# A gated recurrence feeding a SwiGLU block: the recurrence's output made transposed, and carried to the SwiGLU's operand by SBUF transfers

## The chip, the cores and the metric

The kernel runs on one core of a Trainium2 chip. The metric is the device time of one execution in microseconds (us). Five engines run side by side, each through its own instructions in order: TensorE (PE, with its weight loads shown as PEld), VectorE (DVE), ScalarE (ACT), GpSimd (POOL) and SyncE (SP), which here only issues DMA transfers.

## The reference, cut to what matters

```python
batch, n_heads, seq, head_dim = (4, 8, 768, 48)          # q, k, v, f_logit, float32
f = 1.0 / (1.0 + np.exp(-f_logit))
for t in range(S):
    state = f[:, :, t, :, None] * state + np.einsum('bhd,bhe->bhde', k[:, :, t], v[:, :, t])
    y[:, :, t] = np.einsum('bhd,bhde->bhe', q[:, :, t], state)
...
x = np.ascontiguousarray(attn_out.transpose(0, 2, 1, 3)).reshape(B * S, H * D)   # 3072 x 384
g = x @ w_gate                                            # 384 x 1536
silu = g * (1.0 / (1.0 + np.exp(-g)))
val = x @ w_val
return (silu * val @ w_out).astype(np.float32)            # 1536 x 384
```

The three weights arrive as 64-bit floats and are turned into 32-bit ones on the chip.

## The kernel before, in words

The sequence is cut into 6 chunks of 128 steps. A unit is one chunk of one batch; there are 24 units, chunk by chunk, 4 batches in each. For a unit the function `attention` does these things, with a `yield` between them:

- `fTp` (L462): 4 TensorE transposes of the gate logits, two heads at a time; ACT takes the sigmoid into `gates`.
- DVE runs a backward product scan (`tails`, L472) and prepares `starts`.
- `kTp`, `qTp` (L462): 8 transposes; DVE multiplies them by the scans into `kT` (L483) and `qT` (L487). A head occupies 48 of 64 rows: even heads rows 0 to 47, odd heads rows 64 to 111. POOL multiplies the state by the chunk's total decay into `decayed` (L491).
- `sc` (L499): the 128 x 128 score matrix of each head, two heads of a pair side by side in the rows of the array; DVE masks them into `A` (L501). `kt` (L506): 4 transposes of `kT`.
- `y` (L516, L519): for each pair of heads one product of `qT` with `decayed` (128 x 96) and two of `A` with `v` (128 x 48), summed in PSUM; ACT copies the 128 x 384 result into `x` (L522). `dS` (L526): eight products that give the state's update.
- `xTp` (L542): 3 transposes of `x`; ACT copies them into `xT` (L543), where features are rows and the 4 x 128 tokens of a chunk are columns.

A chunk of `xT` (512 tokens) is one block of the SwiGLU, `mlp`: for each of 12 slices of 128 hidden features a `gate` piece and a `val` piece of 3 matmuls each (L564), then 4 `down` pieces, one per batch, of 12 matmuls each (L580, tile `o`). An fp32 matmul shows as two matmul records and two weight loads, a transpose as one.

The first chunk's attention runs alone. After it, `take_turns` mixes the SwiGLU pieces of chunk c with the attention steps of chunk c + 1: after piece i it has issued the share i/n of the steps. `attention_steps` orders these steps so that two units overlap; `parts = [1, 2, 1, 1, 1]` says how many yields go into each of a unit's steps. In the first block `weights()` pieces are mixed in too: each fetches a piece of a 64-bit weight (SP), splits it (ACT) and joins it (DVE, L416 to L420). Where such program order leaves a choice, the tile framework's scheduler settles the order in each engine's queue. SP's queue also holds the loads of `f`, `k`, `q`, `v` of the unit three ahead, in order; outputs go by ACT's queue. PSUM has 4 banks for attention (`bank`) and 4 for the SwiGLU.

Of the kernel before, what the change touches and what calls it, by code (L numbers as in the profile page):

```python
# [9 lines left out]
FP32 = mybir.dt.float32  # L10
# [279 lines left out]
def short_path(ctx, tc, least, judge, q, k, v, f_logit, moe_w_gate, moe_w_val, moe_w_out, out):  # L290
# [26 lines left out]
    att = ctx.enter_context(tc.tile_pool(name="att", bufs=2))  # L317
    ffn = ctx.enter_context(tc.tile_pool(name="ffn", bufs=2))
# [5 lines left out]
    ident = const.tile([128, 128], FP32, tag="ident", name="ident")  # L324
# [51 lines left out]
    vt = {}  # L376
# [69 lines left out]
    xT = {}  # L446

    def rows_of(par):
        return slice(W * par, W * par + D)

    def bank(name):
        return aps.tile([128, 512], FP32, tag="a", name=name)

    def attention(u):
        b, c = units[u]
        fr, kr, qr = (raw[nm][u % NRAW] for nm in "fkq")
        gate, tail, start = (x[u % NROT] for x in (gates, tails, starts))

        def transposed(name, src):
            p = bank(name)  # L460
            for a in range(HP):
                nc.tensor.transpose(p[:, a * C:(a + 1) * C],  # L462
                                    src[:, 2 * a:2 * a + 2, :].rearrange("t r d -> t (r d)"), ident)
            return p.rearrange("p (a t) -> p a t", t=C)

        p = transposed("fTp", fr)
# [4 lines left out]
        n = HP * N1  # L471
# [14 lines left out]
        qT = att.tile([128, HP, C], FP32, tag="qT", name="qT")  # L486
        nc.vector.tensor_tensor(qT, qp, pairs(head)[:, :, 1:N1], ALU.mult)  # L487
# [15 lines left out]
        if c < NCH - 1:  # L503
            p = bank("kt")
# [3 lines left out]
            nc.scalar.copy(kt, p.rearrange("t (h d) -> t h d", d=W))  # L508
        yield


        y = bank("y")
        for a in range(HP):
            both = y[:, 2 * a * D:2 * (a + 1) * D]
            if c:
                nc.tensor.matmul(both, lhsT=qT[:, a, :], rhs=decayed[:, a, :, :].rearrange("p r d -> p (r d)"),  # L516
                                 start=True, stop=False, skip_group_check=True)
            for par in range(2):
                nc.tensor.matmul(both[:, par * D:(par + 1) * D], lhsT=A[:, par, a, :], rhs=vt[u][:, 2 * a + par, :],  # L519
                                 start=(c == 0), stop=True, skip_group_check=True)  # L520
        x = att.tile([128, DM], FP32, tag="x", name="x")
        nc.scalar.copy(x, y[:, 0:DM])  # L522
        if c < NCH - 1:
            p = bank("dS")
            for h in range(H):
                nc.tensor.matmul(p[W * (h % 2):W * (h % 2) + W, (h // 2) * D:(h // 2 + 1) * D],  # L526
                                 lhsT=kt[:, h, :], rhs=vt[u][:, h, :], start=True, stop=True)
# [7 lines left out]
        yield  # L535


        if b == 0:
            xT[c] = ffn.tile([128, KT, TB], FP32, tag="xT", name="xT", bufs=2)
        p = bank("xTp")  # L540
        for i in range(KT):
            nc.tensor.transpose(p[:, i * C:(i + 1) * C], x[:, i * 128:(i + 1) * 128], ident)  # L542
        nc.scalar.copy(xT[c][:, :, b * C:(b + 1) * C], p[:, 0:KT * C].rearrange("p (a t) -> p a t", t=C))  # L543
        yield

    def load_after(u):
# [3 lines left out]
    def attention_steps(c):  # L550

        runs = [attention(c * B + b) for b in range(B)]
        parts = [1, 2, 1, 1, 1]
        order = sorted((2 * b + s, b, n) for b in range(B) for s, n in enumerate(parts))
        return [lambda b=b, n=n: [next(runs[b]) for _ in range(n)] for _, b, n in order]


    def mlp(c):
        h = {}

        def product(w, j, name):
            p = fps.tile([128, 512], FP32, tag="m", name=name)[:, 0:TB]
            for i in range(KT):
                nc.tensor.matmul(p, lhsT=w[:, i, j * 128:(j + 1) * 128], rhs=xT[c][:, i, :],  # L564
                                 start=(i == 0), stop=(i == KT - 1))
            return p

        def gate(j):
            p = product(w_gate, j, "gate")
            h[j] = ffn.tile([128, TB], FP32, tag="h", name="h", bufs=NF + 1)  # L570
            nc.scalar.activation(h[j], p, AF.Silu)  # L571

        def val(j):
            p = product(w_val, j, "val")
            nc.vector.tensor_tensor(h[j], h[j], p, ALU.mult)  # L575

        def down(b):
            p = fps.tile([128, 512], FP32, tag="m", name="o")[:, 0:DM]
            for j in range(NF):
                nc.tensor.matmul(p, lhsT=h[j][:, b * C:(b + 1) * C], rhs=w_out[:, j, :],  # L580
                                 start=(j == 0), stop=(j == NF - 1))
            ob = ffn.tile([128, DM], FP32, tag="ob", name="ob", bufs=3)
            nc.scalar.copy(ob, p)  # L583
            t0 = b * S + c * C
            nc.scalar.dma_start(out=out[t0:t0 + C, :], in_=ob)

        return ([lambda j=j, f=f: f(j) for i in range(0, NF, 2) for f in (gate, val) for j in (i, i + 1)]
                + [lambda b=b: down(b) for b in range(B)])

    def take_turns(first, second):  # L590

        done = 0
        for i, f in enumerate(first):
            f()
            want = (i + 1) * len(second) // len(first)
            for g in second[done:want]:
                g()
            done = want
        for g in second[done:]:
            g()  # L600

    def weights():
        if fetches:
# [10 lines left out]
    mark = traced[-1]  # L614
    keep_warm(5)
    first = [attention(b) for b in range(B)]
    done = [0] * B

# [60 lines left out]
def kernel(  # L679
# [22 lines left out]
    def judge(bank):  # L702
# [46 lines left out]
```

## Time and profile before

| | |
|---|---|
| time, median of 3 runs | 729.62 us (729.58 to 729.69) |
| the profiled execution's own time | 729.66 us |
| its span (first to last instruction) | 727.9 us |
| granted TensorE clock, mean | 0.998 |
| busy: PE, PEld, DVE, ACT, POOL | 718.8, 415.8, 248.9, 185.2, 21.6 us |
| DMA | 38.34 MB, mean 53 GB/s |

A row of the groups view names the line, engine, operation, written and read tiles with their shape, and how many; then the busy time and the mean duration of one in ns; then the idle time of the engine before them and what ended it. A row of the timeline gives start and length in us; consecutive instructions of one kind are merged, and since matmuls are pipelined a merged row ends later than the next one starts. The time that a group takes on the path is therefore read from one row's start to the next row's start.

### The profile page before, as it was taken

What the parts mean: (1) busy time and instruction counts of PE and PEld (TensorE: products, weight loads), DVE (VectorE), ACT (ScalarE), POOL (GpSimd) and SP (SyncE); (2) the same over time, 40 slices, a digit from 0 to 9 for tenths busy, and PEclk for the clock granted to TensorE, in tenths of its full rate; (3) what the DMA queues carried; (4) which work ended last, traced back from release to release, by engine and by line L of the source; (5) the groups of instructions that cost most, each with busy time, mean ns of one, the idle gap of its engine ahead of it and who ended that gap; (6) DMA issues with size and microseconds to landing.
All of it is one profiled execution on the core that took longest, in us unless ns stands there. A gap on an engine that the chain in (4) does not pass through costs nothing.

```text
span 727.9 us, 7635 instructions
## 1 busy us (share of the span) xinstructions
PE 718.8 (99%) x3146; PEld 415.8 (57%) x3146; DVE 248.9 (34%) x405; ACT 185.2 (25%) x272; POOL 21.6 (3%) x43
## 2 busy tenths in 40 slices
PE   8999999999999999999999999999999999999997
PEld 6845555655555665555566555556555566544454
DVE  8799797024234003333202433311333320011100
ACT  2655473032212103323103213301223210100100
POOL 2000000000000000000000000000000000000000
PEclk9999999999999999999999999999999999999999
DMA  9988463112111002211101112010200000000000
GB/s 194 249 224 226 140 172 76 32 35 43 32 33 40 26 23 44 44 23 32 33 23 43 33 33 43 12 32 23 45 1 1 0 1 23 23 0 1 0 23 24
DMA packets 109772, 38.34 MB, mean 53 GB/s; under 512 B 100512, under 2 KB 103584, under 8 KB 109728
## 3 DMA queue, kind: packets, MB, share of 16 engines
q1 hardware_dynamic: 106272, 33.04, 19.5%
q10 hardware_dynamic: 3456, 4.72, 1.8%
q8 instruction: 27, 0.44, 0.2%
q14 instruction: 17, 0.14, 0.1%
HBM read 33.03 MB, written 4.72 MB: 52 GB/s over the span
## 4 chain that ended last, share of the span: by engine, by line
PE 97%; DVE 1%; ACT 1%; DMA 1%; SPq 0%; issue 0%; DVEq 0%
PE o L580 26%; PE val L564 26%; PE gate L564 26%; PE y L519 5%; PE sc L499 4%; PE y L516 3%; PE dS L526 2%; PE kt L506 2%; PE qTp L462 1%; PE kTp L462 1%; PE fTp L462 1%; PE xTp L542 1%; DMA fraw<-in_f_logit_dram 1%; PE idle L340 0%; ACT xT L543 0%; ACT ob L583 0%
## 5 line engine op out<-in xcount | busy, mean ns | idle before, releaser
L564 PE MATMUL gate<-xT,w_gate 128*128 128x512 f32 x432 | 196.4, 596 | 0.8 <-ACT xT L543 0.5
L564 PE MATMUL val<-xT,w_val 128*128 128x512 f32 x432 | 195.7, 595 | 0.1
L580 PE MATMUL o<-w_out,h 128*128 128x384 f32 x576 | 188.8, 487 | 0.0
L580 PEld LDWEIGHTS o<-w_out,h 128*128 128x128 f32 x576 | 108.3, 190 | 73.2 <-issue 0.5
L564 PEld LDWEIGHTS val<-xT,w_val 128*128 128x128 f32 x432 | 79.1, 190 | 86.5 <-issue 84.9
L564 PEld LDWEIGHTS gate<-xT,w_gate 128*128 128x128 f32 x432 | 78.5, 190 | 84.4 <-issue 81.8
L575 DVE TENSOR_TENSOR h<-h,val 128x512 f32<-128x512 f32 x72 | 49.2, 684 | 184.0 <-PE val L564 184.0
L571 ACT ACTIVATE h<-gate 128x512 f32<-128x512 f32 x72 | 42.9, 597 | 205.6 <-PE gate L564 205.4
L472 DVE TENSOR_TENSOR_SCAN tails<-gates,ones 128x516 f32<-128x516 f32 x24 | 29.5, 1231 | 91.5 <-ACT gates L467 91.5
L501 DVE TENSOR_TENSOR A<-sc,causal 128x512 f32<-128x512 f32 x48 | 30.9, 684 | 81.2 <-PE sc L499 81.2
L583 ACT COPY ob<-o 128x384 f32<-128x384 f32 x24 | 11.5, 478 | 183.5 <-PE o L580 183.5
L519 PE MATMUL y<-v,A 128*128 128x48 f32 x384 | 53.5, 267 | 0.4 <-issue 0.2
L519 PEld LDWEIGHTS y<-v,A 128*128 128x128 f32 x384 | 49.7, 192 | 0.8 <-issue 0.4
L491 POOL TENSOR_TENSOR decayed<-state,tails 128x384 f32<-128x384 f32 x20 | 17.4, 868 | 561.8 <-DVE tails L472 561.8
L485 DVE TENSOR_TENSOR_SCAN head<-gates,starts 128x516 f32<-128x516 f32 x24 | 33.4, 1391 | 0.6
L516 PE MATMUL y<-decayed,qT 128*128 128x96 f32 x160 | 32.8, 286 | 0.0
L499 PEld LDWEIGHTS sc<-qT,kT 48*128 48x128 f32 x384 | 23.6, 187 | 15.3 <-issue 13.6
L516 PEld LDWEIGHTS y<-decayed,qT 128*128 128x128 f32 x160 | 25.8, 192 | 8.5 <-issue 6.9
L467 ACT ACT_TABLE_LOAD x20 | 25.7, 1283 | 16.1 <-PE fTp L462 13.5
L499 PE MATMUL sc<-qT,kT 48*128 48x128 f32 x384 | 28.4, 285 | 0.0
L532 DVE TENSOR_TENSOR state<-decayed,dS 64x192 f32<-64x192 f32 x32 | 11.2, 351 | 48.2 <-PE dS L526 47.9
L571 ACT ACT_TABLE_LOAD x20 | 25.7, 1283 | 0.4
(58 smaller groups left out, 350.3 us busy)
## 6 DMA issues: line engine op xcount, KB each, us to landing
fraw<-in_f_logit_dram SPq DMA_DIRECT2D x24, 192.0 KB, 3.1
kraw<-in_k_dram SPq DMA_DIRECT2D x24, 192.0 KB, 3.0
qraw<-in_q_dram SPq DMA_DIRECT2D x24, 192.0 KB, 3.5
v<-in_v_dram SPq DMA_DIRECT2D x24, 192.0 KB, 3.5
w<-in_moe_w_gate_dram SPq DMA_DIRECT2D x6, 768.0 KB, 6.2
w<-in_moe_w_val_dram SPq DMA_DIRECT2D x6, 768.0 KB, 5.9
w<-in_moe_w_out_dram SPq DMA_DIRECT2D x6, 768.0 KB, 4.4
out_dram<-ob ACTq DMA_DIRECT2D x24, 192.0 KB, 1.8
```

Source lines behind the costliest of these rows:

```text
L462: nc.tensor.transpose(p[:, a * C:(a + 1) * C], src[:, 2 * a:2 * a + 2, :].rearrange("t r d -> t (r d)"), ident)
L467: nc.scalar.activation(pairs(gate)[:, :, 1:N1], p, AF.Sigmoid)
L472: nc.vector.tensor_tensor_scan(tail[:, 0:n][:, ::-1], gate[:, 0:n][:, ::-1], ones[:, ::-1], 1.0, op0=ALU.mult, op1=ALU.add)
L485: nc.vector.tensor_tensor_scan(head, gate[:, 0:n], start, 1.0, op0=ALU.mult, op1=ALU.add)
L499: nc.tensor.matmul(sc[par][:, a * C:(a + 1) * C], lhsT=kT[r, a, :], rhs=qT[r, a, :], start=True, stop=True)
L501: nc.vector.tensor_tensor(A[:, par], sc[par].rearrange("p (a t) -> p a t", t=C), causal.unsqueeze(1).broadcast_to((128, HP, C)), ALU.mult)
L516: nc.tensor.matmul(both, lhsT=qT[:, a, :], rhs=decayed[:, a, :, :].rearrange("p r d -> p (r d)"), start=True, stop=False, skip_group_check ...
L519: nc.tensor.matmul(both[:, par * D:(par + 1) * D], lhsT=A[:, par, a, :], rhs=vt[u][:, 2 * a + par, :], start=(c == 0), stop=True, skip_gro ...
L564: nc.tensor.matmul(p, lhsT=w[:, i, j * 128:(j + 1) * 128], rhs=xT[c][:, i, :], start=(i == 0), stop=(i == KT - 1))
L571: nc.scalar.activation(h[j], p, AF.Silu)
L575: nc.vector.tensor_tensor(h[j], h[j], p, ALU.mult)
L580: nc.tensor.matmul(p, lhsT=h[j][:, b * C:(b + 1) * C], rhs=w_out[:, j, :], start=(j == 0), stop=(j == NF - 1))
```

## The change

For chunks 1 to 5 (20 of the 24 units) the operands of the `y` products are swapped: what was streamed is now loaded as weights (48 columns) and the reverse, so that `y` comes out with a head's 48 features as rows (0 to 47 or 64 to 111, as in `kT`) and 128 tokens as columns. ACT copies the two row ranges into `yT`, and ten DMAs per unit on SP's queue move the heads' rows to their places in `xT`: rows h x 48 onward, split where a head crosses a multiple of 128. The `xTp` transposes and their copy stay for the first chunk alone. There the `y` products are as before.

A unit's last two yields are one step now (`parts = [1, 2, 1, 2]`, 16 steps in place of 20), and `take_turns` spreads a chunk's steps over all pieces but the last `rest = 2`.

```diff
+        if b == 0:
+            xT[c] = ffn.tile([128, KT, TB], FP32, tag="xT", name="xT", bufs=2)
         y = bank("y")
-        for a in range(HP):
-            both = y[:, 2 * a * D:2 * (a + 1) * D]
-            if c:
-                nc.tensor.matmul(both, lhsT=qT[:, a, :], rhs=decayed[:, a, :, :].rearrange("p r d -> p (r d)"),
-                                 start=True, stop=False, skip_group_check=True)
+        if c:
+            for a in range(HP):
+                cols = slice(a * C, (a + 1) * C)
+                for par in range(2):
+                    nc.tensor.matmul(y[rows_of(par), cols], lhsT=decayed[:, a, par, :], rhs=qT[:, a, :],
+                                     start=True, stop=False, skip_group_check=True)
+                for par in range(2):
+                    nc.tensor.matmul(y[rows_of(par), cols], lhsT=vt[u][:, 2 * a + par, :], rhs=A[:, par, a, :],
+                                     start=False, stop=True, skip_group_check=True)
+            yT = att.tile([128, HP, C], FP32, tag="x", name="yT")
             for par in range(2):
-                nc.tensor.matmul(both[:, par * D:(par + 1) * D], lhsT=A[:, par, a, :], rhs=vt[u][:, 2 * a + par, :],
-                                 start=(c == 0), stop=True, skip_group_check=True)
-        x = att.tile([128, DM], FP32, tag="x", name="x")
-        nc.scalar.copy(x, y[:, 0:DM])
+                nc.scalar.copy(yT[rows_of(par)], y[rows_of(par)].rearrange("p (a t) -> p a t", t=C))
+            for h in range(H):
+                f = h * D
+                while f < (h + 1) * D:
+                    n = min((h + 1) * D, (f // 128 + 1) * 128) - f
+                    r = W * (h % 2) + f - h * D
+                    nc.sync.dma_start(out=xT[c][f % 128:f % 128 + n, f // 128, b * C:(b + 1) * C],
+                                      in_=yT[r:r + n, h // 2, :])
+                    f += n
...
-        p = bank("xTp")
...
+        if not c:
+            p = bank("xTp")
...
-        parts = [1, 2, 1, 1, 1]
+        parts = [1, 2, 1, 2]
...
-    def take_turns(first, second):
+    def take_turns(first, second, rest):
         done = 0
+        n = len(first) - rest
         for i, f in enumerate(first):
             f()
-            want = (i + 1) * len(second) // len(first)
+            want = min(i + 1, n) * len(second) // n
...
-        take_turns(pieces, attention_steps(c + 1) if c + 1 < NCH else [])
+        take_turns(pieces, attention_steps(c + 1) if c + 1 < NCH else [], 2)
```

At the end of the second SwiGLU block TensorE's queue read so before (`o` are the down pieces, the `y` rows are the fourth batch's next chunk):

```order
L580 MATMUL o<-w_out,h 128x384 x12
L516 MATMUL y<-decayed,qT 128x96
L519 MATMUL y<-v,A 128x48 x2
...
L526 MATMUL dS<-v,kt 64x48 x8
L580 MATMUL o<-w_out,h 128x384 x12
L542 MATMUL xTp<-ident,x 128x128 x3
L462 MATMUL fTp<-ident,fraw_98 128x128 x4
L462 MATMUL kTp<-ident,kraw_95 128x128
L564 MATMUL gate<-xT,w_gate 128x512 x6
```

and now, at the same place:

```order
L598 MATMUL o<-w_out,h 128x384 x12
L520 MATMUL y<-qT,decayed 48x128 x2
L523 MATMUL y<-A,v 48x128 x2
...
L545 MATMUL dS<-v,kt 64x48 x8
L598 MATMUL o<-w_out,h 128x384 x24
L582 MATMUL gate<-xT,w_gate 128x512 x6
L462 MATMUL fTp<-ident,fraw_98 128x128 x4
L582 MATMUL val<-xT,w_val 128x512 x6
L462 MATMUL kTp<-ident,kraw_95 128x128 x4
```

One down piece more stands between the last `y` and the next block's first gate, the `xTp` transposes between them are gone, and the following chunk's first transposes no longer stand ahead of that gate.

SP's queue in the second block, now, with what each transfer waits for (each transfer counts on one of eight semaphores, and waits for the one before it on the same semaphore):

```order
L384 DMA v<-in_v_dram 128x8x48 [waits DMAHW7_49,PE_49]
L533 DMA xT<-yT 48x128 [waits DMAHW0_49,Activation_49]
L533 DMA xT<-yT 48x128 [waits DMAHW1_49,Activation_49]
L533 DMA xT<-yT 32x128 [waits DMAHW2_49]
L533 DMA xT<-yT 16x128 [waits DMAHW3_49]
L533 DMA xT<-yT 48x128 [waits DMAHW4_49]
L533 DMA xT<-yT 48x128 [waits DMAHW5_49]
L533 DMA xT<-yT 16x128 [waits DMAHW6_49]
L533 DMA xT<-yT 32x128 [waits DMAHW7_49]
L533 DMA xT<-yT 48x128 [waits DMAHW0_49]
L533 DMA xT<-yT 48x128 [waits DMAHW1_49]
L382 DMA kraw_96<-in_k_dram 128x8x48 [waits DMAHW2_49,PE_49]
```

A unit's ten transfers stand among the loads of later units, and whatever stands behind them is issued after ACT's copies of that unit.

More of the change, by code (lines that the diff above doesn't have):

```diff
@@ L535, in attention @@
         yield
-        if b == 0:
-            xT[c] = ffn.tile([128, KT, TB], FP32, tag="xT", name="xT", bufs=2)
-        p = bank("xTp")
-        for i in range(KT):
-            nc.tensor.transpose(p[:, i * C:(i + 1) * C], x[:, i * 128:(i + 1) * 128], ident)
-        nc.scalar.copy(xT[c][:, :, b * C:(b + 1) * C], p[:, 0:KT * C].rearrange("p (a t) -> p a t", t=C))
+        if not c:
+            p = bank("xTp")
+            for i in range(KT):
+                nc.tensor.transpose(p[:, i * C:(i + 1) * C], x[:, i * 128:(i + 1) * 128], ident)
+            nc.scalar.copy(xT[c][:, :, b * C:(b + 1) * C], p[:, 0:KT * C].rearrange("p (a t) -> p a t", t=C))
         yield
@@ L598, in take_turns @@
             done = want
-        for g in second[done:]:
-            g()
     def weights():
```

6 lines of the change are left out of this document (added).

## The prediction

> **What bounds the kernel now.** I read the page first, then TensorE's groups, then TensorE's timeline in one steady unit and at a chunk boundary, and last the queues that the new steps join. From the page:
>
> ```profile
> span 727.9 us, 7635 instructions
> PE 718.8 (99%) x3146; PEld 415.8 (57%) x3146; DVE 248.9 (34%) x405; ACT 185.2 (25%) x272; POOL 21.6 (3%) x43
> PE 97%; DVE 1%; ACT 1%; DMA 1%; SPq 0%; issue 0%; DVEq 0%
> ```
>
> TensorE is busy for 99% of the span and carries 97% of the chain that ended last. A change pays by what it takes off TensorE's queue, or costs by what it adds or makes TensorE wait for. The groups that the change touches:
>
> ```profile
> L519 PE MATMUL y<-v,A 128*128 128x48 f32 x384 | 53.5, 267 | 0.4 <-issue 0.2 <-DVE A L501 0.2
> L516 PE MATMUL y<-decayed,qT 128*128 128x96 f32 x160 | 32.8, 286 | 0.0
> L526 PE MATMUL dS<-v,kt 128*64 128x48 f32 x320 | 13.4, 226 | 0.0
> L542 PE MATMUL xTp<-ident,x 128*128 128x128 f32 x72 | 11.8, 275 | 0.0
> ```
>
> The same 48 streamed columns cost 53.5/384 = 139 ns in `y` and 13.4/320 = 42 ns in `dS`. The difference is in the weights: `y` loads 128 columns for each, `dS` 64. A unit on the timeline, start to start:
>
> ```profile
> 307.19 0.49 PE L542 MATMUL xTp<-ident,x 128*128 128x128 f32 x3
> 307.52 5.32 PE L564 MATMUL val<-xT,w_val 128*128 128x512 f32 x12
> 312.77 1.16 PE L499 MATMUL sc<-qT,kT 48*128 48x128 f32 x16
> 313.86 0.66 PE L506 MATMUL kt<-ident,kT 128*128 128x128 f32 x4
> 314.35 2.74 PE L564 MATMUL gate<-xT,w_gate 128*128 128x512 f32 x6
> 316.93 0.60 PE L462 MATMUL fTp<-ident,fraw 128*128 128x128 f32 x4
> ...
> 319.94 0.36 PE L516 MATMUL y<-decayed,qT 128*128 128x96 f32 x2
> ...
> 322.65 0.67 PE L526 MATMUL dS<-v,kt 128*64 128x48 f32 x16
> 323.25 5.42 PE L564 MATMUL val<-xT,w_val 128*128 128x512 f32 x12
> ```
>
> Now a unit's `y` takes 322.65 - 319.94 = 2.71 us for 24 records (0.113 each), `dS` 0.60 and `xTp` 0.33. Six gate records take 2.58, so 512 streamed columns cost 0.43 us and 128 cost about 0.11, as the three transposes show too (0.33/3).
>
> **What the new products cost.** Per unit 16 matmuls, 32 records, each streaming 128 columns through weights of 48 columns. One after another that is 32 x 0.11 = 3.5 us, more than is removed. All rests on whether two of them run at once, one in the array's columns 0 to 63 and one in 64 to 127; the code alternates them. `dS` has this form, and these are its first 2 and first 4 records, cut out by two short windows of the timeline; the third row is `sc`, which alternates between the array's rows:
>
> ```profile
> 322.65 0.26 PE L526 MATMUL dS<-v,kt 128*64 128x48 f32 x2
> 322.65 0.32 PE L526 MATMUL dS<-v,kt 128*64 128x48 f32 x4
> 312.77 0.49 PE L499 MATMUL sc<-qT,kT 48*128 48x128 f32 x4
> ```
>
> Two records of `dS` fit into 0.26 us where one lasts 0.23, so the two start almost together. From the fourth to the sixteenth (0.32 to 0.67) are six pairs in 0.35 us, 0.058 a pair: less than two streams of 48 columns (2 x 0.04). So column pairs do stream at once. `sc` needs 1.16 - 0.49 = 0.67 for six pairs of 128 columns, 0.112 a pair, the price of a single stream. I take 0.110 for a pair of the new `y` (bounds 0.107, the bare stream, and two streams in turn, 0.22): 16 pairs, 1.76 us.
>
> Entering and leaving such a mode costs something. Before `sc`, twelve records that should take 2 x 2.58 = 5.16 take 312.77 - 307.52 = 5.25: 0.09. Its own 1.09 us (to 313.86) is 0.20 more than 8 x 0.112, in which lie a first weight load of 128 columns and the way out. `dS`, with shorter weights, has 0.60 - 8 x 0.058 = 0.14. The new `y` and `dS` share one mode, so they pay once: 0.09 to enter, 0.05 for a 48-column load (estimate, under half of a 128-column one at 0.11), 1.76 + 0.47 of pairs, 0.15 to leave: 2.52 us. Before, both took 323.25 - 319.94 = 3.31. Saved: 0.79 a unit, for 16 units 12.6 us. The last chunk's four units have no `dS`:
>
> ```profile
> 534.87 0.36 PE L516 MATMUL y<-decayed,qT 128*128 128x96 f32 x2
> ...
> 537.48 1.09 PE L564 MATMUL val<-xT,w_val 128*128 128x512 f32 x2
> ```
>
> There 2.61 us become 0.09 + 0.05 + 1.76 + 0.15 = 2.05: 0.56 saved, 2.2 for four. The `xTp` of 20 units go: 20 x 0.33 = 6.6 us. Sum: 21.4 us off TensorE.
>
> [...]
>
> **Chunk boundaries.** At the end of a block TensorE waits for the copy of the last `xTp`:
>
> ```profile
> 273.06 0.49 PE L542 MATMUL xTp<-ident,x 128*128 128x128 f32 x3
> 273.38 0.60 PE L462 MATMUL fTp<-ident,fraw 128*128 128x128 f32 x4
> 273.82 0.27 PE L462 MATMUL kTp<-ident,kraw 128*128 128x128 f32 x1
> 274.17 1.12 PE L564 MATMUL gate<-xT,w_gate 128*128 128x512 f32 x2
> ...
> 629.02 0.27 PE L706 MATMUL row<-idf,low 128*1 128x128 f32 x1
> 629.80 1.12 PE L564 MATMUL gate<-xT,w_gate 128*128 128x512 f32 x2 [0.51 <-ACT xT L543]
> ```
>
> The transpose at 273.82 ends its stream at 273.93, the gate starts at 274.17: 0.24 lost, at four boundaries; at the last one 0.78 - 0.11 = 0.67. Together 1.6 us, which go if `xT` has landed. What is late next is the transfer chain of the chunk's fourth unit: ACT's copies, ten issues on SP, the last landing. Its rows:
>
> ```profile
> L508 ACT COPY kt<-kt 128x512 f32<-128x512 f32 x20 | 11.7, 586 | 44.4 <-PE kt L506 44.4
> L522 ACT COPY x<-y 128x384 f32<-128x384 f32 x24 | 11.5, 478 | 42.3 <-PE y L519 42.2
> L543 ACT COPY xT<-xTp 128x384 f32<-128x384 f32 x24 | 11.4, 479 | 24.1 <-PE xTp L542 24.0
> 66.09 0.37 SPq L382 DMA_DIRECT2D kraw<-in_k_dram  x1
> 66.58 0.50 SPq L382 DMA_DIRECT2D qraw<-in_q_dram  x1
> out_dram<-ob ACTq DMA_DIRECT2D x24, 192.0 KB, 1.8
> w<-in_moe_w_gate_dram SPq DMA_DIRECT2D x6, 768.0 KB, 6.2
> ```
>
> Two copies of 512 columns, 2 x 0.59 = 1.2 us; ten issues, 10 x 0.49 = 4.9; a landing between 1.8 and 6.2, I take 3 since a transfer is 24 KB at most. That is 9 us after `y`. The cover is `dS` and two down pieces; one is 24 `o` records, and the chunk-0 row quoted below gives 11.78 us for 36, so 24 take 7.7: 16 us of cover. With the slowest landing it is still 12.3. If the cover were gone, each microsecond of lateness would cost five. ACT pays 1.18 for 0.96 a unit, on an engine that is 25% busy: nothing. The loads of later units, queued behind the ten transfers on SP, are issued three units ahead of their use: nothing.
>
> **New waits.** The first three gate matmuls now wait on up to 8, 5 and 3 transfer semaphores. A separate wait shows as one short sequencer instruction:
>
> ```profile
> L499 PEldq EVENT_SEMAPHORE  x4: 51/51/51, 9.9 to 26.9; - x4
> PEld sc L499 <- DVE qT L487: 0.8, 1, 0.8
> 34.00:124.00 90.00, 89.89 (x409) 50.52 (x409) 79.42 (x122) 51.29 (x67) 4.03 (x4) 1.00 0.65 175
> 122.84 0.96 DVE L420 CUSTOM_DVE_ANT_0 w_out<-top,up 128x1536 uint16<-128x1536 uint16 x1
> 118.64 11.78 PE L580 MATMUL o<-w_out,h 128*128 128x384 f32 x36
> ```
>
> At 51 ns, 16 of them are 0.8 us a boundary, mostly under running matmuls: I take 0.2, so 1.0 us in all (bounds 0 and 4). With 16 steps in 26 pieces, a unit's `qTp` stands one gate piece (2.58 us) ahead of its `sc` in two units of a chunk, where two to three pieces stood before; DVE must finish `qT` in that time. Such a wait cost 0.8 us once before; I take 0 (to 3 if the first unit of four chunks pays it). In the first block DVE is busy 79.4 of 90 us, and the last weight join ends at 123.80; the down piece needs it after 20 records, at 118.64 + 20 x 0.32 = 125.1. TensorE will come there three units earlier, 3 x 1.1 = 3.4 us, against a slack of 1.3 and 10.6 us of DVE idle time that can close up. I take a loss of 1.0 us (0 to 4.5, the block's whole gain).
>
> Sum: 12.6 + 2.2 + 6.6 + 1.6 - 1.0 - 1.0 = 21.0 us. From the profiled execution's 729.66 (span 727.9 and 1.8 around it; the median, 729.62, is the same) this gives 708.7 us.
>
> **The rivals.**
> - Loads and streams in turn within a pair. A 128-column load limits `y` now at 0.112, so 48 columns cost about 0.042; a pair costs 0.15, 16 pairs 0.64 us more than forecast, 12.8 over 20 units: 721.5 us. For it: nothing in this trace has long streams in column pairs. Against: `dS`. [...]
> - Slower: no overlap of column pairs with long streams, say because the streams share one read path that 48 columns do not fill. `y` then takes 32 x 0.110 = 3.52 in place of 1.76: 20 x 1.76 = 35 us more, 744 us. It decides above a pair price of 0.110 + 21.0/320 = 0.176. Against it: 0.058 a `dS` pair is under two streams in turn.
> - Slower: late transfers. Eight semaphores serve ten transfers, so the ninth waits for the first to land; with a landing L the chain is 1.2 + 2L + 1. It passes 16 us at L = 7 and eats the whole gain (4.2 us at each of five boundaries) at L = 9. At L = 10 it costs 5 x 6.2 = 31: 740 us. No row has L above 6.2.
> - The first block gains nothing, and each new wait costs its bound: 21.4 + 1.6 - 4 - 3 - 4.5 = 11.5 off, 718 us.
> - The change does less than it says: if all transfers landed in time but the gates still waited as before, 1.6 us stay: inside the range.
>
> **How the numbers follow.** Forecast 0.80; loads in turn 0.07; no overlap 0.04; late transfers 0.03; all waits at their bounds 0.06. The forecast's own range runs from 25 us off (pairs at 0.107, 1.0; first load hidden, 1.0; no new waits, 2.0: 704.7) to two of the three new waits at their bounds (23.0 - 4 - 4.5 = 14.5 off: 715). That holds a little over 8 in 10 and is the range. A difference of 0.2% (1.5 us) is what a measurement of this kernel can tell. Faster: 0.80 + 0.07 + 0.06 = 0.93 less a little for transfers that are late by some 4 us, 0.92; same 0.02; slower 0.06.
>
> **What would show it.** Right: `y` at some 1.8 us from its first record to `dS`, pairs at 0.11; no transposes at L560 beyond the first chunk; the first gate of a block right behind the last `o`; the last `xT` transfer landed 4 us or more before it; TensorE's busy time near 698 us. Wrong: `y` records in turn (a unit's `y` at 2.4 or 3.5 us), a gate that waits on a DMA, or a `val`, `sc` or `o` in the first block that waits on DVE.

## The result, and the profile after

The changed kernel takes 710.23 us, the median of 4 runs (707.47 to 711.15), beside 729.65 us for the kernel before in the same session: a ratio of 0.9724, 95% interval 0.9694 to 0.9754. The profiled execution took 707.47 us with a span of 705.7, against 729.66 and 727.9 before. In a second session the changed kernel took 708.25 us (5 runs, 707.84 to 710.96). The forecast for the profiled execution was 708.7, the range 704.7 to 715.

From the page of the changed kernel, the same three rows as before:

```profile
span 705.7 us, 8136 instructions
PE 694.1 (98%) x3246; PEld 388.0 (55%) x3246; DVE 246.3 (35%) x405; ACT 190.7 (27%) x272; POOL 21.6 (3%) x43
PE 83%; DVE 3%; issue 2%; ACT 1%; DMA 1%; ACTq 0%
```

TensorE is busy 24.7 us less (718.8 to 694.1), the span is 22.2 us shorter. So 2.5 us of what was taken off TensorE came back as idle time, and the chain that ended last now passes through DVE for 3%. Its groups:

```profile
L520 PE MATMUL y<-qT,decayed 128*48 128x128 f32 x320 | 31.8, 277 | 0.0
L523 PE MATMUL y<-A,v 128*48 128x128 f32 x320 | 31.0, 273 | 0.0
L499 PE MATMUL sc<-qT,kT 48*128 48x128 f32 x384 | 27.9, 285 | 3.6 <-DVE qT L487 3.5
```

The 640 records of the new `y` are busy for 62.8 us together. The 480 of the old one in the same 20 units, with fewer streamed columns, were busy for 78.4: the 86.3 of both lines in the prediction less 7.9 for the first chunk's 64 records, which the change leaves as they are. The only new idle time stands at `sc`, 3.5 us. TensorE's timeline at the end of the second block, the place of the prediction's boundary:

```profile
240.67 7.91 PE L598 MATMUL o<-w_out,h 128*128 128x384 f32 x24
248.51 0.43 PE L520 MATMUL y<-qT,decayed 128*48 128x128 f32 x4
...
250.29 0.62 PE L545 MATMUL dS<-v,kt 128*64 128x48 f32 x16
250.84 15.75 PE L598 MATMUL o<-w_out,h 128*128 128x384 f32 x48
266.43 4.03 PE L582 MATMUL gate<-xT,w_gate 128*128 128x512 f32 x9
```

`y` takes 250.29 - 248.51 = 1.78 us, each four records 0.218 us (in the timeline they start at 248.76, 248.98 and so on: two pairs of 0.109), `dS` 0.55, and the gate follows the last `o` without a wait. By block, from one block's first gate to the next, before and after (the columns: length; busy time of PE, PEld, DVE, ACT, POOL; granted clock; DMA share; GB/s):

```profile
33.91:154.13 120.22, 120.03 (x537) 69.67 (x536) 80.13 (x124) 54.19 (x74) 4.03 (x4) 1.00 0.51 138
154.13:274.17 120.04, 119.96 (x540) 69.99 (x541) 33.76 (x56) 27.55 (x40) 3.34 (x4) 1.00 0.16 33
...
514.25:629.80 115.55, 115.04 (x456) 65.45 (x456) 31.41 (x51) 25.24 (x36) 3.33 (x4) 1.00 0.05 13
```

```profile
34.03:151.55 117.52, 113.97 (x553) 63.45 (x552) 79.73 (x124) 54.73 (x72) 4.03 (x4) 1.00 0.54 148
151.55:266.43 114.88, 114.88 (x562) 64.45 (x561) 33.24 (x56) 28.71 (x40) 3.33 (x4) 1.00 0.19 42
...
496.18:607.79 111.61, 111.61 (x482) 60.53 (x481) 30.41 (x49) 26.37 (x36) 3.33 (x4) 1.00 0.08 20
```

A steady block gained 5.16 us, the fifth 3.94, the first only 2.70. The change also moved the border between blocks: the next chunk's first four `fTp` and one `kTp`, 0.55 us, stood ahead of a block's first gate before and stand behind it now. In the middle blocks this cancels; without it the first block gained 2.15 and the fifth 4.49. The first block has the same DVE work as before (79.7 us) in a shorter time, and there TensorE waits:

```profile
110.27 2.74 PE L582 MATMUL val<-xT,w_val 128*128 128x512 f32 x6
116.47 1.16 PE L499 MATMUL sc<-qT,kT 48*128 48x128 f32 x16 [3.46 <-DVE qT L487]
```

DVE's queue at that time. The transposes that `kT` and `qT` read were done by about 110.5:

```profile
112.68 0.56 DVE L416 TENSOR_SCALAR top<-top 128x768 f32<-128x768 f32 x1
113.27 0.56 DVE L418 TENSOR_SCALAR top<-top 128x768 int32<-128x768 int32 x1
113.85 0.56 DVE L416 TENSOR_SCALAR top<-top 128x768 f32<-128x768 f32 x1
114.44 0.69 DVE L593 TENSOR_TENSOR h<-h,val 128x512 f32<-128x512 f32 x1
115.04 0.68 DVE L483 TENSOR_TENSOR kT<-kTp,tails 128x512 f32<-128x512 f32 x1
115.64 0.68 DVE L487 TENSOR_TENSOR qT<-qTp,head 128x512 f32<-128x512 f32 x1
```

`kT` and `qT` stand behind the parts of two weight joins and an `h` product that also came late. In the forecast this loss stood at the down piece, with 1.0 us. The transfers of the second block's last unit on the timeline, and how long one of 24 KB takes from issue to landing (the view of DMAs):

```profile
250.51 1.18 ACT L527 COPY yT<-y 48x512 f32<-48x512 f32 x2 [1.42 <-PE y L523]
251.41 6.36 SPq L533 DMA_DIRECT2D xT<-yT  x10
```

```profile
xT<-yT SPq DMA_DIRECT2D x120, 24.0 KB, 1.8
```

The last is issued by 257.8 and lands near 259.6, 6.9 us before the gate at 266.43.

### The profile page after: what moved, and what is told of

Read it like the earlier page. It is cut to its first block, busy times and chain, and to the rows that moved or that the text cites. A ratio compares the mean times of both kernels' runs of the same rounds, so it can differ in the third digit from the quotient of the medians.

```text
span 705.7 us, 8136 instructions
## 1 busy us (share of the span) xinstructions
PE 694.1 (98%) x3246; PEld 388.0 (55%) x3246; DVE 246.3 (35%) x405; ACT 190.7 (27%) x272; POOL 21.6 (3%) x43
## 4 chain that ended last, share of the span: by engine, by line
PE 83%; DVE 3%; issue 2%; ACT 1%; DMA 1%; ACTq 0%
PE o L598 26%; PE val L582 22%; PE gate L582 22%; PE sc L499 3%; PE y L520 2%; PE y L523 2%; PE kt L506 1%; PE fTp L462 1%; PE kTp L462 1%; PE qTp L462 1%; DMA w<-in_moe_w_out_dram 1%; PE dS L545 1%; DVE top L419 0%; ACT top L410 0%; ACT up L408 0%
## 5 line engine op out<-in xcount | busy, mean ns | idle before, releaser
L472 DVE TENSOR_TENSOR_SCAN tails<-gates,ones 128x516 f32<-128x516 f32 x24 | 29.5, 1230 | 116.6 <-ACT gates L467 116.6
L527 ACT COPY yT<-y 48x512 f32<-48x512 f32 x40 | 23.1, 579 | 33.3 <-PE y L523 32.8
L520 PE MATMUL y<-qT,decayed 128*48 128x128 f32 x320 | 31.8, 277 | 0.0
L523 PE MATMUL y<-A,v 128*48 128x128 f32 x320 | 31.0, 273 | 0.0
L520 PEld LDWEIGHTS y<-qT,decayed 128*48 128x48 f32 x320 | 17.8, 123 | 14.1 <-issue 9.5
```

Of the source, the lines that this page charges most:

```text
L472: nc.vector.tensor_tensor_scan(tail[:, 0:n][:, ::-1], gate[:, 0:n][:, ::-1], ones[:, ::-1], 1.0, op0=ALU.mult, op1=ALU.add)
L520: nc.tensor.matmul(y[rows_of(par), cols], lhsT=decayed[:, a, par, :], rhs=qT[:, a, :], start=True, stop=False, skip_group_check=True)
L523: nc.tensor.matmul(y[rows_of(par), cols], lhsT=vt[u][:, 2 * a + par, :], rhs=A[:, par, a, :], start=False, stop=True, skip_group_check=True)
L527: nc.scalar.copy(yT[rows_of(par)], y[rows_of(par)].rearrange("p (a t) -> p a t", t=C))
```

## The experiments

Four questions were open. Is it the pairing that makes the new `y` cheap? What makes TensorE wait in the first block: SP's queue, where the ten transfers hold back the weight fetches behind them (theory A), or DVE, which has the same work in less TensorE time (theory B)? Why do the runs of one kernel differ by up to 3.7 us: a clock that falls after the idle stretch (theory C), or another cause (theory D)? And what are the placing and the merged steps worth? Since the start of the program differs from one execution to the next (the first block's first gate stands between 33.5 and 36.1 us in the profiles; see the last section), single stages are compared by the length of a block, gate to gate, and not by the span.

### The column groups in turn

```diff
-            for a in range(HP):
-                cols = slice(a * C, (a + 1) * C)
-                for par in range(2):
+            for par in range(2):
+                for a in range(HP):
+                    cols = slice(a * C, (a + 1) * C)
...
-                for par in range(2):
```

> The new y products ordered by column group: all eight of the even heads first, then all eight of the odd heads, so that neighbours never stand in different column groups. The same instructions, weights and streams. Theory: the pairs stream at once only because the code alternates them, and nothing else makes the new y cheap. Then 32 records cost 0.11 us each, y takes 3.5 us a unit in place of 1.78, 20 x 1.74 = 35 us more: about 742 to 746. Rival: the gain comes from loading 48 columns of weights in place of 128, or the engine pairs matmuls over a longer distance; then the time stays within 3 us of the changed kernel's, 707 to 714.

733.67 us (10 runs, 731.77 to 735.36), ratio to the kernel before 1.0047 (1.0033 to 1.0060). A steady block takes 120.27 us, 5.39 more than in the changed kernel, 1.35 a unit. Without the alternation the whole change is a small loss, and the rival (cheap because it loads 48 columns) falls. But the 26.6 us of span between the two are not 35. TensorE's timeline in one unit:

```profile
184.42 0.38 PE L522 MATMUL y<-A,v 128*48 128x128 f32 x2
184.63 0.42 PE L520 MATMUL y<-qT,decayed 128*48 128x128 f32 x4
184.85 0.42 PE L522 MATMUL y<-A,v 128*48 128x128 f32 x4
185.11 0.38 PE L520 MATMUL y<-qT,decayed 128*48 128x128 f32 x2
...
185.99 0.27 PE L520 MATMUL y<-qT,decayed 128*48 128x128 f32 x1
185.99 0.32 PE L544 MATMUL dS<-v,kt 128*64 128x48 f32 x2
```

Two records take 0.218 us in turn, 0.109 each, as the forecast's single stream. At 184.63, where the order goes from the even heads to the odd ones, four records fit into the same time: the odd group's first two matmuls started beside the even group's last two, ahead of their place in the order. At 185.99 `dS` runs beside the last `y` in the same way. Eight of the 32 records a unit thus had a neighbour anyway, and `y` with `dS` took 3.68 us in place of 2.33.

### The kernel before with its steps ending early

```diff
+        n = len(first) - 2
...
-            want = (i + 1) * len(second) // len(first)
+            want = min(i + 1, n) * len(second) // n
```

> The kernel before, with only the new placing: a chunk's twenty attention steps end two pieces ahead of the block. The y products, the xTp transposes and their copies are as before. Theory: this part of the change is worth the waits at the boundaries alone, 4 x 0.24 + 0.67 = 1.6 us: about 728.0. Rival: ending earlier also presses the first block's DVE work, and costs there what the boundaries give: 729 to 732.

739.19 us (4 runs, 737.27 to 740.44), ratio 1.0127 (1.0109 to 1.0145): neither the theory nor its rival. By itself the early end costs 9.5 us in the medians, 7.6 in the profiled execution. TensorE's waits:

```profile
PE sc L499 <- DVE qT L487: 5.0, 4, 1.2
PE y L519 <- DVE A L501: 1.7, 2, 1.6
```

Once in each of the four later blocks `sc` waits 1.25 us for `qT`, at the chunk's first unit: twenty steps over 26 pieces put `fTp`, `qTp` and `sc` too close for the chain over ACT and DVE between them. A steady block takes 121.02 us, 0.98 more than before: the wait of 1.25 less the boundary's 0.24. The first block takes 3.9 more: a wait of 1.6 us for `A`, and behind it 6.8 us at a granted clock of 0.50.

### The changed kernel with twenty steps

```diff
-        parts = [1, 2, 1, 2]
+        parts = [1, 2, 1, 1, 1]
```

> The changed kernel with a unit's work in five steps again, the fifth empty, so that twenty steps are spread over the pieces in place of sixteen. TensorE's work is the same. Theory: the early end of the steps cost 9.5 us in the kernel before because twenty steps stood too close, sc behind its qTp by one piece of three matmuls pairs (four waits of 1.2 us on qT, 1.7 us on A); merging two steps is what keeps those waits away. Then four or more waits of about 1 us on qT come back, and with the larger one in the first block the time is 712 to 718. Rival: what hurt there was the transposes of the old output and their copies between the steps; with them gone twenty steps cost nothing, 706 to 711.

717.42 us (5 runs, 714.89 to 720.23), ratio 0.9814 (0.9792 to 0.9837). TensorE's waits:

```profile
PE sc L499 <- DVE qT L487: 7.6, 5, 2.6
PE y L523 <- DVE A L501: 2.1, 1, 2.1
```

The four waits of 1.25 us are back and a steady block takes 116.20 us, 1.32 more, with not one matmul added. So the one line `parts = [1, 2, 1, 2]`, which looks like tidying, is what makes the early end free.

### No cover for the transfers

```diff
-        take_turns(pieces, attention_steps(c + 1) if c + 1 < NCH else [], 2)
+        take_turns(pieces, attention_steps(c + 1) if c + 1 < NCH else [], 0)
```

> The changed kernel with a chunk's steps spread over all pieces (nothing of the block left behind the last step), so that the next block's first gate follows the last unit's y and dS directly. The wait of that gate is the transfer chain itself. Theory: 1.4 us to the copies, 6.4 us of ten issues on SP, 1.8 us to land, less 0.6 us of dS: 8 to 9 us at each of five boundaries, 40 to 45 us, less the first block's wait if that goes (3.5); with the clock's loss behind each gap (some 2.5 us) up to 55. Time 746 to 765. Rival: the scheduler moves other work of TensorE (the next unit's transposes, its sc) into the gap, or the transfers of the earlier units are all that is slow; then below 735.

735.51 us (4 runs, 735.07 to 736.01), ratio 1.0067 (1.0050 to 1.0084): between theory and rival. Without cover the change loses its whole gain, but a boundary costs the second block 3.9 us (the later ones 2.7 to 4.3) and not 8 to 9. TensorE's timeline there:

```profile
276.84 0.66 PE L462 MATMUL fTp<-ident,fraw 128*128 128x128 f32 x4
...
280.50 3.29 PE L582 MATMUL gate<-xT,w_gate 128*128 128x512 f32 x4 [2.10 <-DMA xT<-yT]
283.58 1.43 PE L582 MATMUL val<-xT,w_val 128*128 128x512 f32 x2
284.84 1.45 PE L582 MATMUL gate<-xT,w_gate 128*128 128x512 f32 x3
```

Three groups of transposes fill the first 1.6 us. Then the gate starts at 280.50, when the first heads have landed, while SP issues the last transfer until 283.65: its first product reads only features 0 to 127. Behind a wait of 2.10 us six records take 284.84 - 280.50 = 4.34 us in place of 2.58: the granted clock is 0.50 for some 3.4 us. 2.10 + 1.76 is the 3.9. In the first block, moreover, the down piece waited 5.8 us for `w_out` joins; that block took 128.0 us in place of 117.52, so about a quarter of the 28.5 us between the two profiled spans is not the boundaries'.

### The first block: transfers from another queue

```diff
-                    nc.sync.dma_start(out=xT[c][f % 128:f % 128 + n, f // 128, b * C:(b + 1) * C],
+                    (nc.gpsimd if c == 1 else nc.sync).dma_start(out=xT[c][f % 128:f % 128 + n, f // 128, b * C:(b + 1) * C],
```

> In the first block alone the forty transfers of yT into xT are issued from GpSimd's queue; SP keeps only its loads and the weight fetches. The new 3.46 us wait of TensorE in the first block (sc at 116.47, for DVE's qT) is at stake. Theory A, the queue: ten transfers at 86.31 hold SP for 6.22 us ahead of the w_out fetches, ACT's split at 100.23 starts 3.3 us late for its fetch, and DVE joins too late. Then the wait falls below 1 us, the first block shortens from 117.6 to some 114 us, and the profiled time is about 704. Theory B, compression: the block asks for the same work of DVE in less TensorE time, wherever the fetches are issued. Then the wait stays at 2.5 to 4 us and the time within 1 us of the changed kernel's, 707.5 to 711.

708.07 us (5 runs, 706.46 to 711.22), ratio 0.9695 (0.9676 to 0.9714). The wait is 2.70 us: within the bound of theory B (2.5 to 4). It is 0.76 less than 3.46, but the changed kernel with nothing edited has 2.90 in another execution (next experiment), so a part for A is not shown. Behind the wait the profile shows something else. First the timeline, then windows of 1 us:

```profile
117.19 2.08 PE L499 MATMUL sc<-qT,kT 48*128 48x128 f32 x16 [2.70 <-DVE qT L487]
```

```profile
116.00:117.00 1.00, 0.00 (x0) 0.00 (x0) 1.00 (x2) 0.00 (x0) 1.00 (x3) 0.81 0.11 30
117.00:118.00 1.00, 0.81 (x8) 0.81 (x9) 1.00 (x3) 0.00 (x0) 0.31 (x1) 0.50 0.15 47
...
123.00:124.00 1.00, 1.00 (x3) 0.45 (x3) 0.34 (x1) 0.00 (x0) 0.00 (x0) 0.78 0.00 0
```

A mean of 0.81 over 1 us is 0.38 us at half clock, and 0.78 is 0.44: the granted clock is 0.50 from 116.6 to 123.4, 6.8 us. The first 0.6 us fall into the wait; of the other 6.2 TensorE loses half, 3.1. `sc` takes 2.01 us there, to the start of `kt` at 119.20, in place of 1.09. The first block took 119.71 us, 2.19 more than the changed kernel's, with a shorter wait. That is the bigger part of why this profiled run took 711.22 and the changed kernel's 707.47; the other 1.5 us are the start, since the first gate stands at 35.55 us and not at 34.03.

### The changed kernel again

Nothing is edited.

> The changed kernel once more, nothing edited, beside its variants. Theory C (the idle stretch of the first block lowers the granted clock in some runs, and not in others): the runs spread from 707 to 711, the longer ones with a clock near 0.994. If this profiled run is a long one, its clock is at half for some 5 us right behind the wait, as it was in the run with the first block's transfers on GpSimd's queue (sc took 2.08 us there in place of 1.16), and the rest of the execution is as in the first profile. Theory D (the clock varies for another reason): the low clock lies elsewhere, or spread over the execution.

708.25 us (5 runs, 707.84 to 710.96; clocks 0.998, 0.998, 0.991, 0.994, 0.997), ratio 0.9711 (0.9689 to 0.9734). The profiled run is the 708.25:

```profile
115.82 1.87 PE L499 MATMUL sc<-qT,kT 48*128 48x128 f32 x16 [2.90 <-DVE qT L487]
```

Here the wait was 2.90 us and the clock 0.50 for 3.4 us behind it, from 116.1 to 119.5 (0.55 in the window of 1 us from 116, 0.75 in that from 119). That is half of the stretch above; in the first profile of this kernel a wait of 3.46 us had none. The first block took 118.49 in place of 117.52, 0.97 more, where 1.7 lost to the clock and 0.56 less wait would give 1.1. Theory C has a mechanism: one kind of wait with three outcomes (none, 3.4 us, 6.8 us at half) gives steps of 1.7 and some 3.1 us. It is not the only source of the spread, since the start adds some 1.5 us in some executions, as above. Which of the two made the runs at 710 to 711 is not shown, because the profiles of this kernel are of faster runs.

### The wait filled with dummy matmuls

```diff
         yield
+        if c == 1 and b == B - 1:
+            keep_warm(10)
```

> Ten dummy matmuls (they write nothing that is used) stand in TensorE's queue ahead of the sc that waits 3.46 us in the first block; at 0.22 us each they fill some 2.2 us of that wait. Theory C, the clock: the runs without a profile at 710 to 711 us had a granted clock of 0.993 to 0.995, the profiled one 1.000 at 707.5, and the single idle gap of 3.5 us is what lowers the clock in those runs. Then every run has a clock of 0.998 or more and a time of 707 to 708. Theory D, the clock varies for another reason: then the runs spread as before, 707 to 711, median about 710, with clocks down to 0.993.

706.89 us (5 runs: 706.44, 706.78, 706.89, 706.97, 709.30), ratio 0.9686 (0.9667 to 0.9705). Of the idle time 1.39 us were left. The first block is as long as in the first profile of the changed kernel, 117.48 us, so the dummies bought no time on the path; they took the spread away from four runs in five, with a clock of 0.998 to 1.0. Of the nine runs of the changed kernel five took 709 us or more, here one of five (709.30, clock 0.996). This bears out theory C, on few runs.

### Work taken off DVE: the clamp on GpSimd, and no clamp

In the first kernel GpSimd does the clamp of the six `w_out` joins (L416), in the second it is left out; the two edits:

```diff
-            nc.vector.tensor_scalar(top.bitcast(FP32), top.bitcast(FP32), as_float(0x38000000), as_float(0x47F00000),
+            (nc.gpsimd if shape[2] == DM else nc.vector).tensor_scalar(top.bitcast(FP32), top.bitcast(FP32), as_float(0x38000000), as_float(0x47F00000),
```

```diff
+            if shape[2] != DM:
-            nc.vector.tensor_scalar(top.bitcast(FP32), ...
+                nc.vector.tensor_scalar(top.bitcast(FP32), ...
```

> One of the four operations of each w_out join (the clamp, 0.56 us) goes from VectorE to GpSimd, which is idle there: six of them, 3.3 us off VectorE in the last third of the first block. SP's queue is as in the changed kernel. Theory B, compression (VectorE is out of time in the first block): the wait of 3.46 us falls by 2.5 us or more, to below 1 us, the clock stays at 0.998 or more, and the time is 703.5 to 705. Theory A, the queue (the w_out pieces arrive too late behind the transfers): less work on VectorE changes little, since its joins wait for the pieces; the wait stays above 2.5 us and the time at 707 to 711.

717.36 us (5 runs, 716.78 to 718.45), ratio 0.9821 (0.9805 to 0.9837). What failed was the assumption that the clamp costs nothing on GpSimd. The groups, then TensorE's timeline:

```profile
L416 POOL TENSOR_SCALAR top<-top 128x768 f32<-128x768 f32 x6 | 17.5, 2925 | 18.1 <-ACT top L410 18.1
L418 DVE TENSOR_SCALAR top<-top 128x768 int32<-128x768 int32 x18 | 11.2, 623 | 6.8 <-POOL top L416 6.6
```

```profile
123.10 2.08 PE L499 MATMUL sc<-qT,kT 48*128 48x128 f32 x16 [10.36 <-DVE qT L487]
```

A clamp takes 2.9 us there against 0.56 on DVE. DVE, in order, waits 6.6 us for it, and `qT`, queued behind the joins, comes 7 us later. It says nothing on A against B, but it shows the lever: what stands ahead of `qT` in DVE's queue sets TensorE's wait.

> The clamp of the six w_out joins (0.56 us each on VectorE) is left out, so 3.3 us of VectorE's work in the last third of the first block go and nothing is added on another engine. (It leaves out the limiting of w_out's magnitudes to the range of a 32-bit float.) Moving this operation to GpSimd did not test this: there it took 2.75 to 3.45 us each and the wait grew to 10.4. Theory B, compression: VectorE is the late engine by itself, so the 2.9 to 3.5 us wait falls to below 1.2 us, the clock stays at 0.997 or more in every run, and the time is 703.5 to 706. Theory A, the queue: the joins wait for late pieces, VectorE gets idle time in place of the clamps and the wait stays above 2.3 us, time 706.5 to 711.

708.11 us (5 runs, 707.76 to 711.25), ratio 0.9720 (0.9696 to 0.9744):

```profile
116.84 1.16 PE L500 MATMUL sc<-qT,kT 48*128 48x128 f32 x16 [2.02 <-DVE qT L488]
```

The wait is 2.02 us: between the theories. With 3.3 us of work gone it fell by 1.4 against the first profile of the changed kernel and by 0.9 against the second. One join more stands ahead of `qT` (five now, four before), which takes back a part of what the clamps gave. The first block takes 116.52 us, 1.0 less; the profiled span of 706.0 hides this behind a start that was 1.4 us longer. DVE had 15.85 of 16 us busy from 98 to 114, so it, not its input, was late there. This speaks for theory B; that DVE's load alone makes the whole wait is not shown.

### Joins at other places in the block

Both kernels move the four extra weight pieces of the first block, the second farther than the first:

```diff
-                turns[NF - 1 - i] += 1
+                turns[NF - 3 - i] += 1
```

```diff
-                turns[NF - 1 - i] += 1
+                turns[NF // 2 - 1 - i] += 1
```

> The four extra weight pieces of the first block stand two pairs of slices earlier (at the slices 7 to 10 in place of 9 to 12), all work kept. In VectorE's order the fourth unit's kT and qT then stand ahead of two and a half joins, one more than in the changed kernel. Theory: the wait is VectorE's order and load at the end of the block, which has 4.3 us of idle time between 66 and 82 us that earlier pieces can use; the wait falls by about a join and a half, 3 us or more, to below 0.6 us, time 703.5 to 706. Rival: the pieces can't come earlier, since they are bound by their fetches (DMA busy 0.83 up to 66 us) or by the three buffers of a fetched piece; then some earlier product waits for its weights instead, and the time stays at 706.5 or more.

708.54 us (5 runs, 707.07 to 708.85), ratio 0.9698 (0.9682 to 0.9715).

> The same four extra weight pieces at the slices 3 to 6. In VectorE's order all joins of the first block stand ahead of the fourth unit's kT and qT. Theory: VectorE's idle time between 66 and 82 us is used, the last join ends some 4 us earlier, and no wait is left at sc: 703.5 to 705. Rival (the fetches bind): DMA engines are busy 0.81 to 0.83 in the first 32 us of the block, so the earlier pieces come late, gate and val products at 55 to 80 us wait for joins, and the time is 707 or more.

710.28 us (5 runs, 709.81 to 711.52), ratio 0.9728 (0.9713 to 0.9742). The rivals come true in both: `sc` waits no more, and others do. TensorE's waits in the first of the two, then in the second:

```profile
PE gate L582 <- DVE w_gate L420: 1.7, 1, 1.7
PE val L582 <- DVE w_val L420: 1.3, 1, 1.3
```

```profile
PE val L582 <- DVE w_val L420: 2.2, 1, 2.2
...
PE gate L582 <- DVE w_gate L420: 1.2, 1, 1.2
```

3.0 and 3.4 us of waits in place of 3.46, and first blocks of 117.41 and 120.07 us (at mean granted clocks of 1.00 and 0.99): the loss moved to other places. Some 3 us of the first block were not to be had by these two placings.

### The best version

```diff
+        if c == 1 and b == B - 1:
+            keep_warm(12)
...
-                    nc.sync.dma_start(out=xT[c][f % 128:f % 128 + n, f // 128, b * C:(b + 1) * C],
+                    (nc.gpsimd if c == 1 else nc.sync).dma_start(out=xT[c][f % 128:f % 128 + n, f // 128, b * C:(b + 1) * C],
```

> The first block's transfers from GpSimd's queue (the wait was 2.70 us there) and twelve dummy matmuls, 0.22 us each, 2.6 us, ahead of the sc that waits. Theory C: with the wait filled the clock has no reason to fall in the first block, and the block from its first gate to the next block's takes 119.71 less the half-clock stretch of 6.4 us at half its length, 116.5 us. The only spread left is that of the start, where the twelve dummies take 2.75 us in one profile and 4.12 to 4.44 in others: runs at 706.0 to 706.6 or at 707.4 to 708.3, none above 708.5. Rival D, the low clock has another source than the idle stretch: some of the runs again at 709 to 711.

706.60 us (5 runs: 705.99, 706.47, 706.60, 706.62, 708.15; clocks 0.998 to 1.0), ratio to the kernel before 0.9681 (0.9666 to 0.9696), where the changed kernel in its second session had 0.9711 (0.9689 to 0.9734): the intervals overlap a little, so that it is faster than the changed kernel is likely and not shown. No run is above 708.5, as theory C had it and D did not. Its first block:

```profile
33.94:150.68 116.74, 116.56 (x565) 64.55 (x563) 80.25 (x124) 54.78 (x72) 25.32 (x44) 1.00 0.55 149
```

The block takes 116.74 us (expected 116.5), 0.78 less than in the first profile of the changed kernel and 1.75 less than in the second, where the granted clock was 0.50 for 3.4 us.

## Why the prediction was right, point by point

The result came where the forecast had it, and the main terms came by their mechanism. In the profiled executions 22.2 us went where 21.0 were forecast. That the sum is so near is in part luck: the pairs were sized 1.7 us too small, the boundaries 0.4 too small and the semaphores 1.0 too dear, and against this stands the first block's loss, 1.9 us too small.

- **Pairs at 0.110 us.** Right: 0.109, and 1.78 us a unit against 1.76. The rival of loads and streams in turn, 0.15 a pair, fell: a pair with its two loads came every 0.109 us. The prediction's first reading, 139 against 42 ns because of the weights alone, leaves out the pairing of `dS` that it finds itself further on.
- **`y` and `dS`: 3.31 to 2.52.** Mis-sized: 2.42. The 0.09 to enter is right, and is paid by the record ahead of `y`: 0.52 us in place of 0.43 for a `gate` record, 0.42 in place of 0.32 for an `o`. The rest was too much: `y` took 1.78 for the forecast's 0.05 and 1.76, and `dS` 0.55 for 0.47 of pairs and 0.15 to leave. Saved 0.88 a unit, in the mean over the units, in place of 0.79: 14.1 in place of 12.6 over sixteen. The last chunk's units went from 2.61 to 1.88 each; with the entry, and 0.04 more to leave than before, 0.60 were saved in place of 0.56, together 2.4 in place of 2.2.
- **`xTp`, 6.6 us, and the boundaries, 1.6 us.** Right: `xTp` took 1.31 us of a block's path before and nothing after, and the gate at 266.43 follows the last `o` at once. The boundaries gave 2.0: at four of them the first gate record took 0.53 us before, behind the transposes, and takes 0.43 now.
- **The transfer chain, 9 us under 16 of cover.** Right: from the end of `y` (250.29) to about 259.6 are 9.3 us. Issues cost 0.64 each in place of 0.49, a landing 1.8 in place of 3. The rival of late transfers is real only without cover, and then cheaper than its sum, as the gate needs the first heads alone.
- **Semaphores, 1.0 us.** Nothing: the first gate starts 0.32 us after the last `o` started, as one `o` follows another. The waits themselves ran some 5 us earlier on the weight loads' queue, under the down piece.
- **`qT` ahead of `sc`, 0 (to 3).** Right for the four later blocks, but by the merged steps, which the prediction named only as the rule of sixteen steps in 26 pieces: with twenty the wait is 1.25 us in each of them, and also in the kernel before when its steps end early.
- **The first block, 1.0 us (to 4.5).** The mechanism was named (DVE's idle time closes up, TensorE comes earlier), the size and the place were not: TensorE waited 3.46 us at `sc`, where the kernel before lost some 0.6 in this block, so 2.9 more. The slack of 1.3 us was counted at the down piece, but DVE serves its queue in order (with the clamp on GpSimd it waited 6.6 us, and `qT` with it), and `kT` and `qT` of the fourth unit stood behind the joins. That SP's queue has a part in it is not shown.
- **What no term held.** Behind a wait of 2.90 us (the changed kernel again) the granted clock was 0.50 for 3.4 us, and behind one of 2.70 (transfers from GpSimd's queue) for 6.8, which cost 1.7 us and some 3.1; behind the 3.46 of the first profile it did not fall. It is in no term because the kernel before has no such wait: after its start TensorE's longest is 0.51 us. Together with the start it is of the size of the distance between the profiled 707.47 and the median of 710.23, but for the runs without a profile only their mean clocks speak for it.

The sum, each term read from start to start of the groups over all blocks: 14.1 + 2.4 + 6.6 + 2.0 - 2.9 = 22.2, as the span shows. What stays open: whether `kT` and `qT` moved ahead of the joins in DVE's queue, with nothing else changed, would free the first block; that was not tried.

## What to carry to other kernels

Two fp32 matmuls with 48 columns of weights each, alternated between the two halves of the array's columns, cost one stream here (0.109 us for two of 128 columns); swapping operands so that the narrow side is loaded can be worth a layout change that DMAs then repair, provided that some 9 us of other work lie between. When a block gets shorter, look for the engine that has the same work in it, and at what stands ahead of the urgent instruction in that engine's queue, not only at its busy share. Interleaved steps that must end earlier needed to be fewer and larger here: with twenty of them in 26 pieces the early end cost 9 us in either kernel.

## What the runs showed of the hardware

- **Idle TensorE and its clock.** Behind single waits of 2.1 to 2.9 us the granted clock fell to 0.50 for 3.4 us (2.90 in the changed kernel again; 2.85, 2.10 and 2.36 at gates without cover). Behind one of 1.6 us (the kernel before with early steps), one of 2.70 (transfers from GpSimd's queue) and one of 3.68 (the last gate without cover) it fell for 6.8 us, over two waits of 2.64 and 2.12 us (twenty steps) for 10.2, and around one of 10.36 us (the clamp on GpSimd) for 13.7. Behind waits of 1.65 us (the groups in turn), 1.79 (a gate without cover), 2.02 (no clamp) and 3.46 (the changed kernel) it did not fall. The mean granted clock of the first block was 1.00 in the first profile of the changed kernel, 0.99 in the second, 0.97 with early steps and with transfers from GpSimd's queue, 0.96 with twenty steps and 0.95 with the clamp on GpSimd. The lengths at half clock lie close to one, two, three and four times 3.4 us. What decides whether the clock falls is not shown; the length of the wait alone does not, since it fell behind 2.10 us and not behind 3.46.
- **Order between column groups.** In the kernel with the groups in turn, the other column group's first matmul is among the four records of the row at 184.63, and the first group's last one, which stands ahead of it in the order, is in the next row, 0.22 us later (184.85). So across column groups TensorE did not start its matmuls in the order of its queue here.
- **The start.** The twelve dummy matmuls at the start of the program took 2.75 us in some executions and 4.12 in others. Their row in the first profile of the changed kernel and in that of the kernel without the clamp:

```profile
8.02 2.75 PE L340 MATMUL idle<-blank 128*128 128x512 bf16 x12
```

```profile
8.03 4.12 PE L340 MATMUL idle<-blank 128*128 128x512 bf16 x12
```

The 1.4 us move all that follows. An experiment on one block is read from that block's length, not from the span.
- **GpSimd.** The clamp of 128 x 768 values takes 2.9 us there and 0.56 on DVE, though in the changed kernel GpSimd is idle for 97% of the span.
